# Attention features and a token/channel mixer on one core: the channel mix of batches 1 to 3 in stretches of 512 columns, batch 1's loads among the weights, half of batch 0's features on GpSimd

## The chip, the cores and the metric

One Trainium2 chip, of which the kernel uses 1 core. The metric is the device time of one execution in microseconds (us); of several runs the median is taken. In the names of the profile PE is TensorE (PEld its weight loads), DVE is VectorE, ACT is ScalarE, POOL is GpSimd and SP is SyncE, which here issues every DMA.

## The reference

```
def phi(x):                        # r = 8, so 64 features a head
    a = einsum('rd,bhsd->bhsr', S1, x); b = einsum('rd,bhsd->bhsr', S2, x)
    return (a[..., :, None] * b[..., None, :]).reshape(*x.shape[:-1], 64)
q_p, k_p = phi(q), phi(k)          # q, k, v: 4 batches, 4 heads, 1088 tokens, 32 wide
kv = einsum('bhsf,bhsd->bhfd', k_p, v); z = k_p.sum(axis=2)
x = (q_p @ kv) / (q_p @ z + 1e-6)  # per head, then heads side by side: (4, 1088, 128)
h = relu(x^T @ w_tok1) @ w_tok2    # token mix, 1088 -> 256 -> 1088
u = x + h^T
out = u + relu(u @ w_ch1) @ w_ch2  # channel mix, 128 -> 1536 -> 128
```

All is float32 in and out.

## The kernel before, in words

The weights come as doubles, 128 partitions wide, in pieces: nine tiles of `w_tok1` in pieces 00 to 04, `w_tok2` in 10 to 15, `w_ch1` in 20 to 22, `w_ch2` in 30 to 32. Each piece is turned into float32 words by five operations (`convert`, L256): ACT takes the magnitude (`.abs`, L266) and the tail (`.low`, L270), DVE clamps (L273), shifts (L277) and merges (L280), and POOL adds the tail (L284 where the result is kept as `whole`, L286 where not). Where a product needs full precision out of the faster fp32r matmuls, the words are split into a high and a low half (`divide_weight`, L361): ACT casts the high half (L368), POOL subtracts it to get the low one (L371). Products are then three matmuls: high by high, high by low, low by high.

A batch b goes through these steps. `K` (L385): k is projected on PE (L396), copied by ACT (L406) and multiplied into features `k_p` by DVE (L415), and summed against v on PE (L432) into `kvz`. `Q`: batch 0 makes its query features on PE (L510), with an ACT copy (L514) and a DVE product (L517) for each of six blocks (three stretches of columns, two pairs of heads). Batches 1 to 3 project on PE (L477), copy by ACT (L543), write rows to DRAM (L551), read them back broadcast into `qp` and `br` (L564, L567) and multiply the two on POOL (L577). `A` (mixing, L581): attention `x` on PE (L596), divided by DVE (L607 to L610), split for batches 1 to 3 by ACT (L616) and POOL (L620); first token product (L641 in batch 0, L647 later), relu, transposes; x transposed into PSUM (L672), onto which the second token product is added (L708 in batch 0, L712 later); the sum u is split by ACT into `uh` (L717) and by DVE into `ul` (L721). `U` (channel mix, L732): for a stretch of columns and each of 12 pieces e of the hidden width, three matmuls make `ps_h` (L747), ACT takes the relu as `hh` (L751), DVE the rest as `hl` (L754), and three matmuls add into `ps_o` (L760); at a stretch's end `o_sb` is rebuilt (L777), the sum added (L780) and stored (L783). The stretches are 384, 384 and 320 columns in each batch, so a batch has 3 x 12 x 6 = 216 of these matmuls.

PSUM is three pools of banks: three `ps_a` for all but the channel mix, three `ps_h`, two `ps_o`. `qp`, `br`, `k_sb`, `v_sb` and `k_p` have one buffer each, `q_sb` two; `uh` and `ul` hold a whole batch (1088 columns), two buffers of each.

The order of the instructions on every engine is set when the program is built, by a planner (`Plan.run`, L97): a list scheduler with its own cost for each operation, which takes of the operations that could start soonest the one with the longest chain of cost behind it (`level`), raised for a batch by `BOOST`. Each engine then runs its list strictly in order; a waiting instruction holds up all behind it. SP's list of DMAs is one queue of that kind. `LOADS` gives the order in which the loads of weights and of batch 0 are issued; the loads of the other batches follow behind. Where the planner sees an idle PE ahead it puts in matmuls on the identity (`fill`, L242) that nothing reads.

Of the kernel before, what the change touches and what calls it, by code (L numbers as in the profile page):

```python
# [207 lines left out]
def attn_mixer_kernel(ctx: ExitStack, tc: tile.TileContext, qT, kT, v1, s64, wt1, wt2, wc1, wc2, out):  # L208
    nc = tc.nc
    engines = {"dve": nc.vector, "pool": nc.gpsimd, "act": nc.scalar}  # L210
    bufs = {"c": 4, "tail": 4, "a_sb": 3, "ar": 2, "den": 2, "o_sb": 2, "q_sb": 2, "u": 2, "uh": 2, "ul": 2, "rec": 2, "hid": HID, "hh": HID, "hl": HID, "rows": 2, "ps_a": 3, "ps_h": 3, "ps_o": 2}
# [273 lines left out]
    def queries_on_pe(qp_hold):  # L485
# [16 lines left out]
        for g, (c0, cn) in enumerate(CHUNKS):  # L502
            for p in range(2):
                a_hold, b_hold, ar_hold = Hold("ps_a"), Hold("ps_h"), Hold("ar")
# [10 lines left out]

                def multiply(_, g=g, p=p, cs=cs, cn=cn):
                    nc.vector.tensor_tensor(qp[:, p, cs], t["ar", g, p][:, :cn], t[1, g, p][:, :cn], op=ALU.mult)  # L517
# [63 lines left out]
    def mixing(b, kvz_done, qp_done, qp_hold, boost):  # L581
# [115 lines left out]
        u_hold = Hold("u")  # L697
        u_done, second_done = [], []
        for i, (c0, cn) in enumerate(CHUNKS):
# [14 lines left out]
            def high(_, i=i, c0=c0, cn=cn):  # L714
                if i == 0:
                    box["uh", b], box["ul", b] = new("uh", [P, S], F32R), new("ul", [P, S], F32R)
                nc.scalar.copy(box["uh", b][:, c0:c0 + cn], t["u", i][:, :cn])  # L717

            def low(_, i=i, c0=c0, cn=cn):
                cs = slice(c0, c0 + cn)  # L720
                nc.vector.tensor_tensor(box["ul", b][:, cs], t["u", i][:, :cn], f32(box["uh", b][:, cs]), op=ALU.subtract)  # L721

            s = plan.add(f"{n}.w{i}", {"pe": 6 * (cn / 2.4 + 14) if b else 8 * (cn / 1.2 + 3)}, second, [m, residuals[i]] + [(is_split if b else is_whole)[1, 2 * i + f] for f in range(2)], (), [u_banks[i], hTs_hold], boost)
# [8 lines left out]
    def channel_mix(b, u_done, u_hold):  # L732
        segs = SEGS if not b else [(i, 0, NCH) for i in range(3)]
        o_holds = [Hold("ps_o") for _ in CHUNKS]
        outs = {}
        for i, e0, e1 in segs:
            c0, cn = CHUNKS[i]
            cs = slice(c0, c0 + cn)
            for e in range(e0, e1):
# [3 lines left out]
                def first(_, t=t, e=e, cs=cs, cn=cn):  # L743
                    h_ps = t["h"] = bank("ps_h")
                    uh, ul = box["uh", b], box["ul", b]
                    for m, (l, r) in enumerate(((0, uh), (0, ul), (1, uh))):
                        nc.tensor.matmul(h_ps[:, :cn], lhsT=part(2, at[2][e][0], l, at[2][e][1] * P, P), rhs=r[:, cs], start=(m == 0), stop=(m == 2))  # L747
# [106 lines left out]
```

## Time and profile before

| | us |
|---|---|
| median of 3 runs (lowest, highest) | 235.20 (234.39, 236.41) |
| profiled execution, its own time | 237.45 |
| its span, first to last instruction | 235.7 |
| PE, busy in the span | 225.1 |
| DVE, busy | 141.6 |
| ACT, busy | 116.9 |
| POOL, busy | 76.1 |

Times within the profile are counted from the span's start. The groups give the busy time of the instructions of one line and their mean duration; a PE instruction's duration runs from its start to the end of its way through the array, so that consecutive matmuls overlap and the time one adds to a stream is read from the distance of their starts (the chain of waits gives that). The waits name what ended an idle time; an engine's timeline gives its instructions in order. The granted TensorE clock is 1.000.

### The profile page before, as it was taken

What the parts mean: (1) busy time and instruction counts of PE and PEld (TensorE: products, weight loads), DVE (VectorE), ACT (ScalarE), POOL (GpSimd) and SP (SyncE); (2) the same over time, 40 slices, a digit from 0 to 9 for tenths busy, and PEclk for the clock granted to TensorE, in tenths of its full rate; (3) what the DMA queues carried; (4) which work ended last, traced back from release to release, by engine and by line L of the source; (5) the groups of instructions that cost most, each with busy time, mean ns of one, the idle gap of its engine ahead of it and who ended that gap; (6) DMA issues with size and microseconds to landing.
All of it is one profiled execution on the core that took longest, in us unless ns stands there. A gap on an engine that the chain in (4) does not pass through costs nothing.

```text
span 235.7 us, 4804 instructions
## 1 busy us (share of the span) xinstructions
PE 225.1 (95%) x1891; PEld 207.0 (88%) x1891; DVE 141.6 (60%) x280; ACT 116.9 (50%) x262; POOL 76.1 (32%) x76
## 2 busy tenths in 40 slices
PE   7799998799998999999998999999999999999994
PEld 7477765699886999989997999989999999999993
DVE  1598994987876356563656355548357456555653
ACT  4577379975623445443443344444443354444451
POOL 1224469898866410000066410100062611000000
PEclk9999999999999999999999999999999999999999
DMA  6999940269741000049951000015931000010000
GB/s 205 416 403 402 408 189 0 50 192 203 170 149 35 2 0 30 1 116 212 164 169 43 3 0 14 16 40 141 164 119 36 3 0 28 0 36 0 3 35 28
DMA packets 8279, 24.88 MB, mean 106 GB/s; under 512 B 960, under 2 KB 2624, under 8 KB 8256
## 3 DMA queue, kind: packets, MB, share of 16 engines
q1 hardware_dynamic: 8256, 24.57, 34.5%
q8 instruction: 15, 0.25, 0.5%
q14 instruction: 8, 0.07, 0.1%
HBM read 21.50 MB, written 3.06 MB: 104 GB/s over the span
## 4 chain that ended last, share of the span: by engine, by line
PE 57%; DMA 21%; DVE 7%; ACT 4%; SPq 4%; issue 4%; POOL 3%; POOLq 0%; DVEq 0%
PE ps_o L760 22%; PE ps_h L747 22%; DMA br<-rows 12%; DMA doubles<-wt 4%; PE ps_a L647 4%; DMA doubles<-wc 4%; PE ps_a L712 4%; PE ps_a L596 3%; DVE c L273 2%; POOL qp L577 2%; ACT halves L368 2%; SPq L567 1%; SPq L249 1%; PE ps_a L672 1%; DVE hl L754 1%
## 5 line engine op out<-in xcount | busy, mean ns | idle before, releaser
L754 DVE SCALAR_TENSOR_TENSOR hl<-ps_h,hh 128x384 fp32r<-128x384 f32 (+1 forms) x144 | 76.1, 533 | 63.2 <-ACT hh L751 62.6
L751 ACT ACTIVATE hh<-ps_h 128x384 fp32r<-128x384 f32 (+1 forms) x144 | 68.0, 474 | 66.9 <-PE ps_h L747 58.5
L747 PE MATMUL ps_h<-uh,halves 128*128 128x384 f32 (+1 forms) x288 | 93.9, 334 | 2.1 <-DVE hl L754 1.5
L760 PE MATMUL ps_o<-hh,halves 128*128 128x384 f32 (+1 forms) x288 | 72.7, 333 | 0.9 <-POOL halves L371 0.5
L747 PEld LDWEIGHTS ps_h<-uh,halves 128*128 128x128 f32 x288 | 53.8, 188 | 4.8 <-DVE hl L754 2.2
L760 PEld LDWEIGHTS ps_o<-hh,halves 128*128 128x128 f32 x288 | 50.3, 188 | 2.5 <-POOL halves L371 1.0
L747 PE MATMUL ps_h<-ul,halves 128*128 128x384 f32 (+1 forms) x144 | 47.2, 328 | 0.1
L760 PE MATMUL ps_o<-hl,halves 128*128 128x384 f32 (+1 forms) x144 | 47.2, 328 | 0.0
L577 POOL TENSOR_TENSOR qp<-qp,br 128x544 f32<-128x544 f32 x12 | 16.2, 1364 | 59.2 <-DMA br<-rows 33.4
L747 PEld LDWEIGHTS ps_h<-ul,halves 128*128 128x128 f32 x144 | 27.1, 189 | 0.5 <-DVE ul L721 0.3
L760 PEld LDWEIGHTS ps_o<-hl,halves 128*128 128x128 f32 x144 | 27.1, 188 | 0.1
L777 POOL TENSOR_TENSOR o_sb<-uh,ul 128x384 f32<-128x384 f32 (+1 forms) x12 | 11.6, 966 | 44.2 <-DVE ul L721 29.1
L284 POOL TENSOR_TENSOR whole<-c,tail 128x512 int32<-128x512 int32 (+3 forms) x11 | 11.8, 1080 | 19.7 <-DVE c L280 18.9
L266 ACT ACTIVATE c<-doubles 128x512 f32<-128x512 f32 (+3 forms) x17 | 10.2, 614 | 6.9 <-POOL whole L284 5.1
L273 DVE TENSOR_SCALAR c<-c 128x512 f32<-128x512 f32 (+3 forms) x17 | 11.9, 718 | 2.5 <-ACT c L266 2.5
L371 POOL TENSOR_TENSOR halves<-whole,halves 128x512 fp32r<-128x512 f32 (+3 forms) x11 | 11.9, 1098 | 0.7 <-ACT halves L368 0.7
L620 POOL TENSOR_TENSOR xl<-x,xh 128x384 fp32r<-128x384 f32 x9 | 9.0, 1011 | 9.3 <-ACT xh L616 9.3
L596 PEld LDWEIGHTS ps_a<-kvz,qp 128*64 128x64 f32 x288 | 9.2, 137 | 3.0 <-issue 1.9
L415 DVE TENSOR_TENSOR k_p<-ps_a,a_sb 128x1024 f32<-128x1024 f32 (+1 forms) x12 | 10.7, 949 | 1.3 <-ACT a_sb L406 1.3
L721 DVE TENSOR_TENSOR ul<-ps_a,uh 128x384 fp32r<-128x384 f32 (+1 forms) x12 | 6.4, 533 | 8.5 <-ACT uh L717 8.5
L596 PE MATMUL ps_a<-kvz,qp 128*64 128x66 f32 x288 | 10.4, 225 | 0.8 <-POOL qp L577 0.8
L277 DVE TENSOR_SCALAR ps_h<-c 128x512 int32<-128x512 int32 (+3 forms) x17 | 10.3, 612 | 0.1
(69 smaller groups left out, 243.7 us busy)
## 6 DMA issues: line engine op xcount, KB each, us to landing
qp<-rows SPq DMA_DIRECT2D x6, 544.0 KB
br<-rows SPq DMA_DIRECT2D x12, 272.0 KB
doubles<-wc SPq DMA_DIRECT2D x6, 512.0 KB
v_sb<-v SPq DMA_DIRECT2D x4, 594.0 KB
k_sb<-kT SPq DMA_DIRECT2D x4, 576.0 KB
q_sb<-qT SPq DMA_DIRECT2D x4, 544.0 KB
doubles<-wt SPq DMA_DIRECT2D x4, 512.0 KB
doubles<-wt SPq DMA_DIRECT2D x4, 384.0 KB
```

What stands on the lines that cost most here:

```text
L273: nc.vector.tensor_scalar(f32(t["c"]), f32(t["c"]), LEAST, MOST, op0=ALU.max, op1=ALU.min)
L277: nc.vector.tensor_scalar(t["ps"], t["c"], 3, 0x3FFFFFFF, op0=ALU.logical_shift_left, op1=ALU.bitwise_and)
L284: engines[e].tensor_tensor(dst(), t["c"], t["tail"], op=ALU.add)
L371: engines[e].tensor_tensor(halves[w, i][:, 1], f32(whole[w, i] if w < 2 else t["c"]), f32(halves[w, i][:, 0]), op=ALU.subtract)
L415: nc.vector.tensor_tensor(t["k_p"][:pn, t0 * H:t1 * H], a.unsqueeze(3).broadcast_to([pn, n, R, R]), t["sb", t0][:pn, :n].unsqueeze(2).broa ...
L577: engines[e].tensor_tensor(qp[:, p, cs], qp[:, p, cs], t["br"][:, p, cs], op=ALU.mult)
L596: nc.tensor.matmul(x_ps[c:c + 64, o:o + 2 * (D + 1)], lhsT=qp[:, p, s0 + c:s0 + c + 64], rhs=kvz_all[b % 2][:, p, :], start=True, stop=True,)
L747: nc.tensor.matmul(h_ps[:, :cn], lhsT=part(2, at[2][e][0], l, at[2][e][1] * P, P), rhs=r[:, cs], start=(m == 0), stop=(m == 2))
L751: nc.scalar.activation(t["hh"][:, :cn], t["h"][:, :cn], AF.Relu)
L754: nc.vector.scalar_tensor_tensor(t["hl"][:, :cn], t["h"][:, :cn], 0.0, f32(t["hh"][:, :cn]), op0=ALU.max, op1=ALU.subtract)
L760: nc.tensor.matmul(outs[i][:, :cn], lhsT=part(3, at[3][e][0], l, at[3][e][1] * P, P), rhs=r[:, :cn], start=(e == 0 and m == 0), stop=(e == ...
L777: engines[e].tensor_tensor(outs["sb", i][:, :cn], f32(box["uh", b][:, cs]), f32(box["ul", b][:, cs]), op=ALU.add)
```

## The change

Seven edits, of which the planner then makes a new order for all engines.

- **Stretches of 512.** Batch 0 keeps 384, 384 and 320. The 3264 columns of batches 1 to 3 are taken as one row and cut into 512 x 5, 448 and 256, so stretches run over the border of two batches. `uh`, `ul`, `hh`, `hl` and `o_sb` become tiles of 512 columns, five `uh` and five `ul` of them. A second-product chunk that lies in two stretches is split by two ACT and two DVE operations (`evict`), and a stretch that lies in two batches is stored by two DMAs.
- **Loads.** q1, k1 and v1 are issued among the weights (behind 30, 13 and 31) and not behind them.
- **GpSimd features.** Of the six blocks of batch 0's query features three, those of the second pair of heads, are multiplied by POOL. It can't read PSUM, so ACT copies both factors; `ar` has three buffers.
- **Single leads.** A table adds to or takes from the level of single operations.
- In batches 1 to 3 the three groups of the attention matmuls stand together as one step, behind the third transposition of the batch before.
- The planner's time for the first load, for a landing, and for batch 0's second product are other numbers.
- `u_done` is a list for each stretch, so a stretch waits for its own pieces alone.

The diff, cut to its core:

```diff
-LOADS = "00 q k 01 v 02 03 04 10 11 20 30 12 13 21 31 14 15 22 32".split()
+LOADS = "00 q0 k0 01 v0 02 03 04 10 11 20 30 q1 12 13 k1 21 31 v1 14 15 22 32".split()
+WIDE = 512
+def _spans():
+    spans = [((0, c0, cn),) for c0, cn in CHUNKS]
+    at = S
+    for n in (512, 512, 512, 512, 512, 448, 256):
...
+ON_POOL = {(0, 1), (1, 1), (2, 1)}
+LEAD = {
+    "A0.d2": -2500.0,
+    "A0.t2": -30000.0,
+    "A0.w1": 7000.0,
...
+    "K3.p": 27000.0,
...
+    "w21.lo": -111500.0,
+}
-            op.level += op.boost
+            op.level += op.boost + LEAD.get(op.name, 0.0)
-        dma, mode = 1680.0, 0
+        dma, mode = 2800.0, 0
-                op.end = dma + 1200
+                op.end = dma + (1200 if op.bytes > 100000 else 0)
-    bufs = {... "ar": 2, ... "u": 2, "uh": 2, "ul": 2, ...}
+    bufs = {... "ar": 3, ... "u": 5, "uh": 5, "ul": 5, ...}
+                def copy_b(_, g=g, p=p, cn=cn):
+                    t["br", g, p] = new("ar", [P, 384])
+                    nc.scalar.copy(t["br", g, p][:, :cn], t[1, g, p][:, :cn])
+                def multiply_both(_, g=g, p=p, cs=cs, cn=cn):
+                    nc.gpsimd.tensor_tensor(qp[:, p, cs], t["ar", g, p][:, :cn], t["br", g, p][:, :cn], op=ALU.mult)
...
+            elif g == 0:
+                attended = plan.add(f"{n}.x", {"pe": 18 * 117.0}, lambda _: [f(_) for f in attends], [kvz_done] + sum(qp_done.values(), []), x_banks, [qp_hold], boost, 1, order=free)
...
+        def evict(k, i, s, src, dst, cn):
+            def high(_):
+                if ("uh", k) not in box:
+                    box["uh", k], box["ul", k] = new("uh", [P, WIDE], F32R), new("ul", [P, WIDE], F32R)
+                nc.scalar.copy(box["uh", k][:, dst:dst + cn], t["u", i][:, src:src + cn])
...
-    def channel_mix(b, u_done, u_hold):
-        segs = SEGS if not b else [(i, 0, NCH) for i in range(3)]
+    def channel_mix(segs):
...
+                    uh, ul = box["uh", i], box["ul", i]
                     for m, (l, r) in enumerate(((0, uh), (0, ul), (1, uh))):
-                        nc.tensor.matmul(h_ps[:, :cn], lhsT=part(...), rhs=r[:, cs], start=(m == 0), stop=(m == 2))
+                        nc.tensor.matmul(h_ps[:, :cn], lhsT=part(...), rhs=r[:, :cn], start=(m == 0), stop=(m == 2))
...
+                for b, c0, m in SPANS[i]:
+                    def store(_, i=i, b=b, c0=c0, m=m, d0=d0):
+                        nc.sync.dma_start(out[b][:, c0:c0 + m], outs["sb", i][:, d0:d0 + m])
...
-            q_loaded[b + 1] = load_q(b + 1, [prev], BOOST[b + 1])
-            k_loaded[b + 1] = load_k(b + 1, [q_loaded[b + 1]], BOOST[b + 1])
-            v_loaded[b + 1] = prev = load_v(b + 1, [k_loaded[b + 1]], BOOST[b + 1])
+            for get, known in by_kind.values():
+                if b + 1 not in known:
+                    prev = known[b + 1] = get(b + 1, [prev], BOOST[b + 1])
```

What the planner made of it, at three places. First PE's list just ahead of batch 0's channel mix, which begins with the first row on `ps_h<-uh`. Lines of the changed kernel are other numbers: L438 and L474 are batch 1's key projection and sums (L396 and L432 before), L702 and L785 batch 0's token products, L733 and L742 transposes, L519 a query projection, L820 and L833 the channel mix. Before:

```order
L708 MATMUL ps_a<-whole_409,hTl 128x384
L708 MATMUL ps_a<-whole_414,hTl 128x384
L245 MATMUL ps_o<-ident 128x128 x5
L708 MATMUL ps_a<-whole_459,hTl 128x384
L708 MATMUL ps_a<-whole_468,hTl 128x384
L747 MATMUL ps_h<-uh,halves_456 128x384
```

Changed:

```order
L438 MATMUL ps_a<-s_c,k_sb 64x64 x18
L702 MATMUL ps_a<-whole_326,x 128x256 x2
L702 MATMUL ps_a<-whole_376,x 128x256
L286 MATMUL ps_o<-ident 128x128 x3
L742 MATMUL ps_a<-ident,h 128x128 x2
L733 MATMUL ps_a<-ident,x 128x128 x3
L785 MATMUL ps_a<-whole_409,hTl 128x384
L785 MATMUL ps_a<-whole_427,hTl 128x384
L733 MATMUL ps_a<-ident,x 128x128 x3
L474 MATMUL ps_a<-v_sb,k_p 64x66 x36
L785 MATMUL ps_a<-whole_479,hTl 128x384
L785 MATMUL ps_a<-whole_563,hTl 128x384
```

Batch 1's keys and sums, which stood among the first groups of the channel mix, now stand ahead of it; so does, some rows earlier, batch 1's query projection. `whole_468` and `whole_563` are the same piece of weights, 13.

Second DVE's list up to the merge of that piece (`c<-doubles_92`). Before:

```order
L280 SCALAR_TENSOR_TENSOR c<-doubles_89,ps_h 128x512
L277 TENSOR_SCALAR ps_h<-c 128x384 x2
L280 SCALAR_TENSOR_TENSOR c<-doubles_91,ps_h 128x384
L273 TENSOR_SCALAR c<-c 128x512
L280 SCALAR_TENSOR_TENSOR c<-doubles_92,ps_h 128x384
```

Changed:

```order
L321 SCALAR_TENSOR_TENSOR c<-doubles_91,ps_h 128x384
L457 TENSOR_TENSOR k_p<-ps_a,a_sb 128x1024 x2
L457 TENSOR_TENSOR k_p<-ps_a,a_sb 128x256
L314 TENSOR_SCALAR c<-c 128x384
L314 TENSOR_SCALAR c<-c 128x512 x2
L318 TENSOR_SCALAR ps_h<-c 128x384
L318 TENSOR_SCALAR ps_h<-c 128x512
L321 SCALAR_TENSOR_TENSOR c<-doubles_92,ps_h 128x384
```

Batch 1's key features, one clamp more and one shift of 512 more now stand ahead of that merge; three of batch 0's products (L517) are gone from the rows above.

Third POOL's list behind the add of that piece (`whole_563`), changed:

```order
L325 TENSOR_TENSOR whole_563<-c,tail 128x384
L327 TENSOR_TENSOR c<-c,tail 128x512 x2
L411 TENSOR_TENSOR halves_583<-c,halves_583 128x512
L327 TENSOR_TENSOR c<-c,tail 128x512
L411 TENSOR_TENSOR halves_626<-c,halves_626 128x512
L411 TENSOR_TENSOR halves_654<-c,halves_654 128x512
L327 TENSOR_TENSOR c<-c,tail 128x512
L411 TENSOR_TENSOR halves_690<-whole_156,halves_690 128x512
L411 TENSOR_TENSOR halves_724<-c,halves_724 128x512
L327 TENSOR_TENSOR c<-c,tail 128x512
L632 TENSOR_TENSOR qp<-qp,br 128x544
L411 TENSOR_TENSOR halves_771<-c,halves_771 128x512
```

The halves that are made from `c` are the channel mix's weights, those from `whole` the token mix's. Before, nine subtractions for the token weights (00 to 04 and 10 to 13) stood among and ahead of the channel weights' later pieces; now all but one stand behind them, and batch 1's feature products (L632, `qp<-qp,br`) stand among them.

More of the change, by code (lines that the diff above doesn't have):

```diff
@@ L210, in attn_mixer_kernel @@
     engines = {"dve": nc.vector, "pool": nc.gpsimd, "act": nc.scalar}
-    bufs = {"c": 4, "tail": 4, "a_sb": 3, "ar": 2, "den": 2, "o_sb": 2, "q_sb": 2, "u": 2, "uh": 2, "ul": 2, "rec": 2, "hid": HID, "hh": HID, "hl": HID, "rows": 2, "ps_a": 3, "ps_h": 3, "ps_o": 2}
+    bufs = {"c": 4, "tail": 4, "a_sb": 3, "ar": 3, "den": 2, "o_sb": 2, "q_sb": 2, "u": 5, "uh": 5, "ul": 5, "rec": 2, "hid": HID, "hh": HID, "hl": HID, "rows": 2, "ps_a": 3, "ps_h": 3, "ps_o": 2}
     const = ctx.enter_context(tc.tile_pool(name="const", bufs=1))
@@ L584, in mixing @@
         x_hold, xs_hold = Hold("x"), Hold("xs")
-        divided, split = [], []
+        divided, split, attends = [], [], []
+        x_banks = [Hold("ps_a") for _ in range(3)]
         for g in range(3):
-            ps = Hold("ps_a")
+            ps = x_banks[g]
             def attend(_, g=g):
@@ L712, in second @@
                         nc.tensor.matmul(u_ps[:, :cn], lhsT=t[l][:, f, :], rhs=part(1, 2 * i + f, r, 0, cn), start=False, stop=(k == 6), skip_group_check=True)
[L714 to L723, printed above, removed]
-            second_done.append(s)
-            hi = plan.add(f"{n}.uh{i}", act(cn), high, [s], [u_hold] if i == 0 else (), [u_banks[i]] + ([u_hold] if i else []), boost, order=u_done[:1])
-            u_done += [plan.add(f"{n}.ul{i}", dve(cn), low, [hi], (), [u_banks[i], u_hold], boost)]
-        return mixed, second_done, u_done, u_hold, residuals
+            s = plan.add(f"{n}.w{i}", {"pe": 6 * (cn / 2.4 + 14) if b else 4 * (cn / 1.2 + 3)}, second, [m, residuals[i]] + [(is_split if b else is_whole)[1, 2 * i + f] for f in range(2)], (), [u_banks[i], hTs_hold], boost)
+            second_done.append(s)
+            for k, parts in enumerate(SPANS):
+                d0 = 0
+                for pb, p0, pn in parts:
+                    lo, n_ = max(c0, p0), min(c0 + cn, p0 + pn) - max(c0, p0)
+                    if pb == b and n_ > 0:
+                        evict(k, i, s, lo - c0, d0 + lo - p0, n_)
+                    d0 += pn
+        return second_done, residuals
     chain = {"f": None, "s": None}
-    def channel_mix(b, u_done, u_hold):
-        segs = SEGS if not b else [(i, 0, NCH) for i in range(3)]
-        o_holds = [Hold("ps_o") for _ in CHUNKS]
-        outs = {}
+    def channel_mix(segs):
+        o_holds, outs = {}, {}
         for i, e0, e1 in segs:
-            c0, cn = CHUNKS[i]
-            cs = slice(c0, c0 + cn)
+            cn = sum(m for _, _, m in SPANS[i])
+            o_hold = o_holds.setdefault(i, Hold("ps_o"))
+            n = f"U{i}"
             for e in range(e0, e1):
@@ L762, in channel_mix @@
                 cost = 3 * (cn / 2.4 + 14)
-                n = f"U{b}"
-                f = plan.add(n + ".f", {"pe": cost}, first, [u_done[i], is_split[2, at[2][e][0]]], [ps], [u_hold], 0.0, 0, 2 * cost, [chain["f"]])
+                f = plan.add(n + ".f", {"pe": cost}, first, u_done[i] + [is_split[2, at[2][e][0]]], [ps], [u_holds[i]], 0.0, 0, 2 * cost, [chain["f"]])
                 chain["f"] = f
@@ L767, in channel_mix @@
                 m = plan.add(n + ".l", dve(cn), low, [m], (), [ps, hid])
-                s = plan.add(n + ".s", {"pe": cost}, second, [m, is_split[3, at[3][e][0]]], [o_holds[i]] if e == 0 else (), [hid] + ([o_holds[i]] if e else []), 0.0, 0, 2 * cost, [chain["s"]])
+                s = plan.add(n + ".s", {"pe": cost}, second, [m, is_split[3, at[3][e][0]]], [o_hold] if e == 0 else (), [hid] + ([o_hold] if e else []), 0.0, 0, 2 * cost, [chain["s"]])
                 chain["s"] = s
```

88 lines of the change are left out of this document (61 added, 27 removed).

## The prediction, made before the changed kernel ran

> **What bounds the kernel now.** First the page's busy times and shares of the chain, then the windows, cut where batch 0's channel mix begins (35.14) and where batch 1's first token product ends (80.7).
>
> ```profile
> PE 225.1 (95%) x1891; PEld 207.0 (88%) x1891; DVE 141.6 (60%) x280; ACT 116.9 (50%) x262; POOL 76.1 (32%) x76
> 0.00:35.14 35.14, 32.04 (x289) 24.21 (x289) 26.60 (x56) 21.02 (x47) 13.02 (x20) 1.00 0.88 339
> 35.14:80.89 45.75, 42.33 (x382) 36.72 (x381) 32.30 (x61) 27.96 (x65) 37.80 (x34) 1.00 0.41 103
> 80.89:232.40 151.51, 150.69 (x1225) 146.07 (x1224) 82.24 (x162) 67.90 (x152) 25.26 (x23) 1.00 0.22 53
> L245 PE MATMUL ps_o<-ident 128*128 128x128 f32 x50 | 8.7, 339 | 1.4 <-POOL ident masks.py:199 1.4
> GB/s 205 416 403 402 408 189 0 50 192 203 170 149 35 2 0 30 1 116 212 164 169 43 3 0 14 16 40 141 164 119 36 3 0 28 0 36 0 3 35 28
> ```
>
> Three stages. In the last, 151.5 us, PE is busy 150.7: matmuls alone set its length. In the middle one PE has holes and POOL is the fullest other engine, 37.8 of 45.75. In the first, PE is full only by name: 50 of its matmuls are filler (8.7 us), and DVE, 26.6 of 35.1 and without a rest from 10 us on, sets the pace. So the end moves by three things: PE's work behind 35.14, PE's waits there, and the moment at which the channel mix begins.
>
> **The change, part by part.** *Stretches of 512.* The chain of waits shows what one group of consecutive matmuls adds to PE's stream: 6 of 320 columns, 3 of 384, 18 of 256.
>
> ```profile
> 222.08 0.88 PE ps_h L747 x6
> 205.84 0.52 PE ps_h L747 x3
> 131.07 2.13 PE ps_a L647 x18
> ```
>
> That is 146.7, 173.3 and 118.3 ns each. From 320 to 384 a column costs 0.417 ns and 13.3 ns stay as a fixed part; so 512 should cost 226.7 and 448 200.0. Batches 1 to 3 pass each stretch in 72 matmuls. Before: 6 x 173.3 + 3 x 146.7 = 1480 ns; changed: 5 x 226.7 + 200.0 + 118.3 = 1452. Difference 28 ns x 72 = **-2.0 us**. The trace has no 512; along the line from 256 to 384 (0.43 a column) it is 228.3 and the gain 1.4; if the fixed part vanished at 512 the gain would be 6.8. I take 2.0, as 320 and 384 are the same instruction at the same place. DVE's and ACT's part of a group grows to some 0.68 and 0.60 us by the rows of 384 and 320, under PE's 1.36 for the pair of groups, so PE stays the longest.
>
> By the Trainium skill, page "TensorE: Matmul & The Clock Gate", section "Back-to-back issue gap", an isolated matmul costs N/2.4 + 2.5 ns, but a sustained stream at N = 512 runs at some 131 ns each. The first would make 384 columns 162.5 ns, and the row above says 173.3.
>
> *Work moved ahead of the channel mix.* Batch 1's query projection (L477), key projection (L396) and sums (L432) stood behind 35.14:
>
> ```profile
> 35.14 0.63 PE L747 MATMUL ps_h<-uh,halves 128*128 128x384 f32 x1
> 37.34 1.14 PE L477 MATMUL ps_a<-q_sb,s_rows 128*64 128x272 f32 x8
> 46.73 1.27 PE L396 MATMUL ps_a<-s_c,k_sb 128*64 128x64 f32 x36
> 50.65 2.32 PE L432 MATMUL ps_a<-v_sb,k_p 128*64 128x66 f32 x72
> ```
>
> 1.14 + 1.27 + 2.32 = 4.7. Their loads now come among the weights and PE does them where it did filler: **-4.7 us**, if the first stage doesn't grow. (Batch 2's query and key projections come forward into the middle stage; that only changes places.) The three loads are some 1.7 MB, 4 us at the 403 GB/s of the row above, and make later weights as much later. That costs nothing: all loads are over when GB/s falls to 0 (slice 7 of 5.9 us, from 35 on), and five of the six channel pieces got their add on POOL behind 33.3 (L286 x5 in POOL's groups below), so they lay waiting.
>
> *The start of the channel mix.* It waits for piece 13: merge on DVE, add on POOL, second token product on PE.
>
> ```profile
> 10.22 0.55 DVE L517 TENSOR_TENSOR qp<-ar,ps_h 128x384 f32<-128x384 f32 x1 [1.91 <-PE ps_h L510]
> 15.74 0.48 DVE L517 TENSOR_TENSOR qp<-ar,ps_h 128x320 f32<-128x320 f32 x1
> 10.69 0.42 DVE L273 TENSOR_SCALAR c<-c 128x512 f32<-128x512 f32 x1
> 11.75 2.68 DVE L415 TENSOR_TENSOR k_p<-ps_a,a_sb 128x1024 f32<-128x1024 f32 x3
> 27.49 2.13 DVE L273 TENSOR_SCALAR c<-c 128x512 f32<-128x512 f32 x2
> 32.72 0.54 DVE L280 SCALAR_TENSOR_TENSOR c<-doubles,ps_h 128x384 int32<-128x384 int32 x1
> 33.19 0.68 DVE L277 TENSOR_SCALAR ps_h<-c 128x512 int32<-128x512 int32 x1
> 27.25 2.15 POOL L284 TENSOR_TENSOR whole<-c,tail 128x384 int32<-128x384 int32 x2 [2.94 <-DVE c L280]
> ```
>
> The merge starts at 32.72; DVE's list ahead of it loses three products (2 x 0.55 + 0.48 = 1.6) and gains batch 1's key features (2.68), a clamp (0.42) and a shift (0.68): 2.2 us more. To that come waits. Two clamps at 27.49 took 2.13 where alone they take about 0.8: they stood behind POOL's adds at 27.25. The change puts three products of POOL, about 1.0 us each, into this stage, and three ACT copies (0.42 to 0.48) ahead of words that DVE wants. I put 1.1 us on that: **+3.3 us**. From below: nothing, if the 2.2 go where DVE waited anyway (the rows show 1.9 at 10.22 and 1.3 at 27.49). From above: each product holds a clamp for its whole 1.0 and the copies stand in line, 2.2 + 3.0 + 1.4 = 6.6.
>
> The Trainium skill, page "SBUF — State Buffer", section "Who interferes with whom", has the rule that speaks against GpSimd features: DVE in a two-port mode and GpSimd lock each other out for a whole instruction. By this, the trace agrees at 27.49, and the dear end would be the right one.
>
> *Waits of the middle stage.*
>
> ```profile
> 38.90 0.44 PE L760 MATMUL ps_o<-hh,halves 128*128 128x384 f32 x1 [0.42 <-ACT hh L751]
> 39.86 0.45 PE L760 MATMUL ps_o<-hh,halves 128*128 128x384 f32 x1 [0.53 <-POOL halves L371]
> 43.90 0.44 PE L747 MATMUL ps_h<-uh,halves 128*128 128x384 f32 x1 [1.33 <-DVE hl L754]
> 73.54 0.41 PE L747 MATMUL ps_h<-uh,halves 128*128 128x320 f32 x1 [0.60 <-ACT uh L717]
> 69.11 0.92 PE L596 MATMUL ps_a<-kvz,qp 128*64 128x66 f32 x24
> 74.55 1.62 PE L596 MATMUL ps_a<-kvz,qp 128*64 128x66 f32 x48
> 70.26 1.63 PE L708 MATMUL ps_a<-whole,hTl 128*128 128x320 f32 x4 [0.23 <-POOL whole L284]
> 80.60 0.28 PE L647 MATMUL ps_a<-halves,xl 128*128 128x256 f32 x1
> 125.39 0.81 PE L596 MATMUL ps_a<-kvz,qp 128*64 128x66 f32 x20 [0.76 <-POOL qp L577]
> ```
>
> From 35.14 to the next start after 80.60 (80.7) are 45.6 us. In it lie 48 groups of 384 (25.0), 4 of 320 (1.8), the 4.7 above, second product (1.6), attention (0.92 + 1.62), first token product (27 x 0.118 = 3.2): 38.8. So 6.8 are waits, one small transposition and what alternating shapes cost. In the new POOL list the channel weights' halves come ahead of the token weights', so the waits at 39.86 and 43.90 and their like shrink; but the second query projection now wants a PSUM bank that `ul` of the second stretch gives back, behind five conversions on DVE, about 1.8 us, and the first output group again waits for the half of piece 30, about 0.5. With 1.4 for transposition and shapes 3.7 stay: **-3.1 us** (between 0, the sum unchanged, and -5). The wait at 125.39 goes, since batch 2's reads are now issued as soon as batch 1's attention is done, some 35 us ahead of use: **-0.8**.
>
> What hides the rest: POOL. Behind the add of piece 13 it has, up to batch 1's feature products, one add of 384, five adds and four halves of 512, one half of a token piece; up to batch 1's first `xl`, 21 us more.
>
> ```profile
> L371 POOL TENSOR_TENSOR halves<-c,halves 128x512 fp32r<-128x512 f32 x6 | 7.7, 1292 | 0.9 <-ACT halves L368 0.9
> L286 POOL TENSOR_TENSOR c<-c,tail 128x512 int32<-128x512 int32 x5 | 6.4, 1289 | 0.2
> L371 POOL TENSOR_TENSOR halves<-whole,halves 128x512 fp32r<-128x512 f32 x4 | 5.3, 1339 | 0.7 <-ACT halves L368 0.7
> L371 POOL TENSOR_TENSOR halves<-whole,halves 128x384 fp32r<-128x384 f32 x4 | 4.1, 1066 | 0.0
> L577 POOL TENSOR_TENSOR qp<-qp,br 128x544 f32<-128x544 f32 x4 | 5.5, 1382 | 2.7 <-issue 2.3 <-DMA br<-rows 0.4
> L620 POOL TENSOR_TENSOR xl<-x,xh 128x384 fp32r<-128x384 f32 x3 | 3.0, 1009 | 2.6 <-ACT xh L616 2.6
> ```
>
> From the merge's end at 36.6 that is 1.1 + 6.4 + 5.2 + 1.3 = 14.0 and some 0.9 of waits: feature products due at 51.5, first `xl` done at 72.8. PE comes there at 38.4 + 32.9 (the 38.8 less 4.7, less the token product and one group, with batch 2's two projections for 2.4) + 3.7 = 75.0. POOL is 2.2 us early: nearly a second bound.
>
> **The sum**: -2.0 - 4.7 - 3.1 - 0.8 + 3.3 = -7.3 us against the span of 235.7, so 228.4. The profiled execution took 237.45 with what lies around its span, but the runs' median is 235.20; taken off that, **227.9 us**. The last stretch is 256 and not 320; its end (one DVE add, one store) I leave as it is.
>
> **Rivals.** (1) *The front slips further*: start +6.6, waits unchanged but for the 0.8. Then -2.0 - 4.7 - 0.8 + 6.6 = -0.9: 234.3, no measurable change. For it: DVE has no rest there and the port waits are real; against: the dear end needs each product to hit a clamp. (2) *Batch 1's feature products hold POOL's list*. They stand ahead of piece 32's half and of all token halves, and their reads on SP stand behind the load of v2, which waits for batch 1's sums.
>
> ```profile
> 48.54 0.58 SPq L564 DMA_DIRECT2D qp<-rows  x1
> 53.01 0.34 SPq L249 DMA_DIRECT2D v_sb<-v  x1
> 60.41 1.36 POOL L577 TENSOR_TENSOR qp<-qp,br 128x544 f32<-128x544 f32 x1 [0.42 <-DMA br<-rows]
> 66.71 2.67 POOL L577 TENSOR_TENSOR qp<-qp,br 128x544 f32<-128x544 f32 x2 [2.29 <-issue]
> ```
>
> Before, 11.9 us passed from issue to first use. From some 37.3, when the sums are done, that gives 49.2, due 51.5. Past 53.7 (51.5 and POOL's 2.2) each us costs one, and past 61.0 the gain is gone; if they took twice their time and a little, to 64, it is 10.3: 238.2, slower than before by 1.3%. For it: POOL's list is strictly in order, and the second pair of reads took 18.2 us. Against: the second pair is due 6 us behind the first. (3) *The changed order helps nothing but the moved work*: waits stay at 6.8, start +3.3: -2.0 - 4.7 - 0.8 + 3.3 = -4.2: 231.0. (4) *The fixed part of a matmul doesn't show at 512*: the stretches give 6.8 and not 2.0: 223.1. Against it: 320 and 384 both carry it. The Trainium skill's section named above would have nearly that (2.5 ns left), and its 131 ns would take far more off; the trace's 173.3 for 384 speaks against both.
>
> **How the numbers follow.** Chances: forecast 0.66, rival 1 0.10, rival 2 0.07, rival 3 0.16, rival 4 0.01. A run of this kernel tells about 1% from no change (232.8 and below is faster, above 237.6 slower). The forecast, rival 3 and 4 are faster, 0.83, with 0.02 of rival 1; rival 2 is half slower (0.04), half same. So faster 0.85, same 0.11, slower 0.04. The range: down by the start at no cost and the waits at -5 gives 222.7, both together are unlikely, 223.5; up to rival 3 and halfway to rival 1, 232.5.
>
> **What would show it.** Right: matmuls of 512 at 227 ns each; the first on `ps_h<-uh` at about 38.4; L438 and L474 ahead of it; batch 1's token product done near 78.2; behind it PE without holes. Wrong: a start past 41, POOL waiting for `br<-rows` past 54, or 512 columns at 235 ns and more, which would eat the gain of the stretches.

## The result, and the profile after

| | before | changed | forecast |
|---|---|---|---|
| median, us | 235.20 | 227.33 (227.18 to 227.35, 4 runs) | 227.9 (223.5 to 232.5) |
| profiled execution, us | 237.45 | 227.31 | |
| its span, us | 235.7 | 225.5 | 228.4 |

The ratio is 0.9665, with a 95% interval of 0.962 to 0.9711. A second set of runs beside other kernels gave 227.19 and 0.9634 (0.96 to 0.9668); one of its six executions took 432.66 us, with matmuls of 512 columns 446 ns apart, and is left out of the ratio. The total came out as forecast; its terms did not.

The changed kernel's busy times, and its windows, cut where batch 0's channel mix begins (37.17) and where batch 1's first token product ends (74.90; the columns are the stretch, its length, then PE, PEld, DVE, ACT and POOL busy, granted clock, DMA share, GB/s):

```profile
PE 217.6 (96%) x1735; PEld 187.6 (83%) x1735; DVE 135.4 (60%) x256; ACT 113.1 (50%) x246; POOL 78.6 (35%) x77
0.00:37.17 37.17, 33.16 (x393) 25.77 (x393) 29.19 (x60) 25.53 (x59) 17.71 (x25) 1.00 0.90 345
37.17:74.90 37.73, 36.99 (x305) 34.41 (x304) 29.44 (x58) 25.26 (x60) 34.98 (x31) 1.00 0.47 127
74.90:222.30 147.40, 147.40 (x1042) 127.39 (x1040) 76.34 (x139) 62.28 (x128) 25.88 (x22) 1.00 0.18 48
```

The front grew by 2.0 us, the middle shrank from 45.75 to 37.7, the last stage from 151.5 to 147.4. PE has no hole left behind 74.90, as forecast (the forecast had this end of the token product near 78.2), and POOL is busy for 93% of the middle stage, against 83% before.

Next PE's timeline around the start of the mix (start, length, instruction, how many, and in brackets an idle time with what ended it):

```profile
21.16 1.14 PE L519 MATMUL ps_a<-q_sb,s_rows 128*64 128x272 f32 x8
27.44 1.27 PE L438 MATMUL ps_a<-s_c,k_sb 128*64 128x64 f32 x36
33.82 2.32 PE L474 MATMUL ps_a<-v_sb,k_p 128*64 128x66 f32 x72
36.07 1.56 PE L785 MATMUL ps_a<-whole,hTl 128*128 128x384 f32 x4
37.17 0.63 PE L820 MATMUL ps_h<-uh,halves 128*128 128x384 f32 x1
38.92 1.14 PE L519 MATMUL ps_a<-q_sb,s_rows 128*64 128x272 f32 x8
44.37 0.44 PE L820 MATMUL ps_h<-uh,halves 128*128 128x384 f32 x1 [0.74 <-DVE hl L827]
```

Batch 1's query projection, key projection and sums (L519, L438, L474) lie ahead of 37.17, and they and the second token product run right up to it: at the start PE itself is what was waited for. DVE's timeline has the merge of piece 13 (the first of the two at 33.99) and the first `ul`, which ends at 35.6; POOL's has that piece's add, over at 35.6 as well. Both are 1.6 us ahead of the start. The other rows are DVE's clamps between 19 and 25 us, and on POOL the three new products (L564) and the adds beside those clamps:

```profile
19.44 1.14 DVE L314 TENSOR_SCALAR c<-c 128x256 f32<-128x256 f32 x2
22.55 1.51 DVE L314 TENSOR_SCALAR c<-c 128x384 f32<-128x384 f32 x2
33.99 1.14 DVE L321 SCALAR_TENSOR_TENSOR c<-doubles,ps_h 128x384 int32<-128x384 int32 x2
35.05 0.55 DVE L768 TENSOR_TENSOR ul<-ps_a,uh 128x384 fp32r<-128x384 f32 x1
12.21 1.00 POOL L564 TENSOR_TENSOR qp<-ar 128x384 f32<-128x384 f32 x1 [2.62 <-ACT ar L557]
15.21 1.02 POOL L564 TENSOR_TENSOR qp<-ar 128x384 f32<-128x384 f32 x1 [1.99 <-ACT ar L557]
17.65 2.51 POOL L325 TENSOR_TENSOR whole<-c,tail 128x512 int32<-128x512 int32 x2 [0.18 <-DVE c L321]
20.68 0.87 POOL L564 TENSOR_TENSOR qp<-ar 128x320 f32<-128x320 f32 x1 [0.52 <-ACT ar L557]
22.71 1.06 POOL L325 TENSOR_TENSOR whole<-c,tail 128x384 int32<-128x384 int32 x1 [0.19 <-DVE c L321]
34.61 1.00 POOL L325 TENSOR_TENSOR whole<-c,tail 128x384 int32<-128x384 int32 x1 [2.74 <-DVE c L321]
```

The chain of waits gives the price of the new stretches, three matmuls of 512 and then six of 448:

```profile
190.55 0.70 PE ps_h L820 x3
199.57 1.23 PE ps_h L820 x6
```

That is 233 and 205 ns a matmul; the starts of consecutive 512 lie 234 ns apart (median of 360). The forecast had 226.7 and 200.0.

PE's named waits behind the start, first of before, then of the changed kernel (total, times, longest):

```profile
PE ps_h L747 <- DVE hl L754: 1.5, 2, 1.3
PE ps_a L596 <- POOL qp L577: 0.8, 1, 0.8
PE ps_h L747 <- ACT uh L717: 0.6, 1, 0.6
PE ps_o L760 <- POOL halves L371: 0.5, 1, 0.5
PE ps_o L760 <- ACT hh L751: 0.4, 1, 0.4
PE ps_a L708 <- POOL whole L284: 0.2, 1, 0.2
```

```profile
PE ps_h L820 <- DVE hl L827: 0.7, 1, 0.7
```

4.0 us became 0.7. POOL's timeline shows the two marks of rival 2, batch 1's first feature product and its `xl`:

```profile
50.07 1.36 POOL L632 TENSOR_TENSOR qp<-qp,br 128x544 f32<-128x544 f32 x1
69.51 2.99 POOL L676 TENSOR_TENSOR xl<-x,xh 128x384 fp32r<-128x384 f32 x3
```

The product didn't wait for its reads and started at 50.07 (due 51.5). The first of the three `xl` was done at 70.5 (forecast 72.8); PE came to it at 71.6 (forecast 75.0), so POOL was only 1.1 us ahead, nearly the second bound that the forecast had seen.

**An account for all kernels.** To compare kernels whose lists differ, I count each matmul behind the first one on `ps_h<-uh` at its kind's usual distance of starts (fp32r of 512, 448, 384, 320, 256 columns: 234, 204, 174, 147, 117 ns; the rest likewise). What the time up to the last matmul holds beyond that is "rest": named waits, and many small delays, above all where kinds of matmul alternate. The rest of "attention split" and of the first "384, 384, 320" also holds what a lowered clock cost. From the profiled executions, us:

| kernel | median | start | work behind | rest behind | end | span |
|---|---|---|---|---|---|---|
| before | 235.2 | 35.1 | 184.4 | 12.4 | 3.7 | 235.7 |
| changed | 227.3 | 37.2 | 180.7 | 4.1 | 3.6 | 225.5 |
| old loads | 229.8 | 32.7 | 186.2 | 5.4 | 3.6 | 227.9 |
| features on DVE | 230.0 | 34.8 | 186.2 | 3.6 | 3.6 | 228.1 |
| no leads | 231.8 | 34.1 | 186.2 | 6.0 | 3.6 | 229.9 |
| these three undone | 232.3 | 34.8 | 186.2 | 5.9 | 3.6 | 230.4 |
| and 384, 384, 320 | 232.3 | 34.5 | 185.7 | 6.3 | 4.2 | 230.6 |
| 384 late | 228.0 | 37.1 | 180.2 | 5.0 | 3.7 | 226.1 |
| attention split | 231.4 | 37.9 | 180.7 | 8.0 | 3.6 | 230.2 |
| 384, 384, 320 | 246.6 | 38.3 | 180.2 | 23.0 | 4.1 | 245.6 |
| same, one lead less | 231.8 | 38.8 | 180.2 | 6.9 | 4.1 | 230.0 |

Before's profiled execution was 2.25 us above its median; if that lies in its rest, the rest was 10.1 in a usual run. A start is good to some 0.8 us: four profiled executions with the same lists ahead of it (384 late, changed, the changed kernel with a stream behind its end, attention split) have it at 37.1, 37.2, 37.5 and 37.9.

By distances of starts, eight single waits of 0.36 to 1.49 us make 5.9 us of before's rest; they are the seven named above and one on `ul`. With "384, 384, 320" and the three edits undone, three such waits make 1.4, in the changed kernel one makes 1.0. So of the 8.3 that the rest fell by, some 4.8 are single waits that went.

### The profile page after: what moved, and what is told of

Read it like the earlier page. It is cut to its first block, busy times and chain, and to the rows that moved or that the text cites. A ratio compares the mean times of both kernels' runs of the same rounds, so it can differ in the third digit from the quotient of the medians.

```text
span 225.5 us, 4427 instructions
## 1 busy us (share of the span) xinstructions
PE 217.6 (96%) x1735; PEld 187.6 (83%) x1735; DVE 135.4 (60%) x256; ACT 113.1 (50%) x246; POOL 78.6 (35%) x77
## 4 chain that ended last, share of the span: by engine, by line
PE 79%; DVE 8%; DMA 7%; SPq 1%; issue 1%; POOL 1%; ACT 1%; DVEq 0%
PE ps_o L833 31%; PE ps_h L820 31%; PE ps_a L708 4%; DMA doubles<-wt 4%; PE ps_a L789 4%; PE ps_a L652 3%; DMA qp<-rows 3%; PE ps_a L474 2%; DVE c L314 2%; DVE c L321 2%; DVE ps_h L318 1%; PE ps_a L733 1%; SPq L290 1%; DVE k_p L457 1%; PE ps_a L438 1%
## 5 line engine op out<-in xcount | busy, mean ns | idle before, releaser
L827 DVE SCALAR_TENSOR_TENSOR hl<-ps_h,hh 128x512 fp32r<-128x512 f32 (+4 forms) x120 | 73.0, 611 | 61.6 <-ACT hh L824 60.7
L824 ACT ACTIVATE hh<-ps_h 128x512 fp32r<-128x512 f32 (+4 forms) x120 | 64.2, 536 | 69.2 <-PE ps_h L820 56.2
L820 PE MATMUL ps_h<-uh,halves 128*128 128x512 f32 (+4 forms) x240 | 86.2, 366 | 0.7 <-DVE hl L827 0.7
L833 PE MATMUL ps_o<-hh,halves 128*128 128x512 f32 (+4 forms) x240 | 67.4, 362 | 0.0
L820 PEld LDWEIGHTS ps_h<-uh,halves 128*128 128x128 f32 x240 | 44.9, 188 | 7.4 <-DVE hl L827 1.2
L833 PEld LDWEIGHTS ps_o<-hh,halves 128*128 128x128 f32 x240 | 42.9, 188 | 5.6
L833 PE MATMUL ps_o<-hl,halves 128*128 128x512 f32 (+4 forms) x120 | 43.4, 361 | 0.0
L820 PE MATMUL ps_h<-ul,halves 128*128 128x512 f32 (+4 forms) x120 | 43.2, 360 | 0.0
L632 POOL TENSOR_TENSOR qp<-qp,br 128x544 f32<-128x544 f32 x12 | 16.2, 1369 | 44.7 <-DMA br<-rows 44.7
L833 PEld LDWEIGHTS ps_o<-hl,halves 128*128 128x128 f32 x120 | 22.5, 188 | 3.4 <-DVE hl L827 0.5
L820 PEld LDWEIGHTS ps_h<-ul,halves 128*128 128x128 f32 x120 | 22.6, 188 | 2.5
L849 POOL TENSOR_TENSOR o_sb<-uh,ul 128x512 f32<-128x512 f32 (+4 forms) x10 | 11.3, 1131 | 36.5 <-DMA outT<-o_sb 22.7
L311 ACT ACTIVATE tail<-doubles 128x512 int32<-128x512 uint32 (+3 forms) x17 | 10.4, 618 | 1.2 <-DMA doubles<-wt 1.2
```

The lines of the kernel that those rows point to most:

```text
L632: engines[e].tensor_tensor(qp[:, p, cs], qp[:, p, cs], t["br"][:, p, cs], op=ALU.mult)
L824: nc.scalar.activation(t["hh"][:, :cn], t["h"][:, :cn], AF.Relu)
L827: nc.vector.scalar_tensor_tensor(t["hl"][:, :cn], t["h"][:, :cn], 0.0, f32(t["hh"][:, :cn]), op0=ALU.max, op1=ALU.subtract)
L833: nc.tensor.matmul(outs[i][:, :cn], lhsT=part(3, at[3][e][0], l, at[3][e][1] * P, P), rhs=r[:, :cn], start=(e == 0 and m == 0), stop=(e == ...
L849: engines[e].tensor_tensor(outs["sb", i][:, :cn], f32(box["uh", i][:, :cn]), f32(box["ul", i][:, :cn]), op=ALU.add)
```

## The experiments

Theory A: fp32r matmuls cost by the column, so stretches of 512 give nothing; the gain is work moved ahead of the mix and waits that went with the new order. Rival B: wide stretches are worth the forecast's 2 us, and 234 ns comes from something beside them.

**The changed kernel again**, as control.

> The changed kernel itself, once more beside the two runs with other stretches, so that all three have the same runs of before to stand against. Both theories: 227.3 us, ratio 0.967.

227.19 us, 0.9634 (0.96 to 0.9668): as expected.

**The price of a width.** The edit, behind the kernel's end (`stream(n, 24)` issues 24 fp32r matmuls of n columns):

```diff
+    for n in (512, 448, 384, 320, 256, 512):
+        stream(n, 24)
...
+    for _ in range(10):
+        nc.scalar.copy(d1, src_ps)
+        nc.vector.tensor_scalar_add(d2, src2_ps, 1.0)
+    stream(512, 24)
```

> The changed kernel, and behind its end 24 matmuls each of 512, 448, 384, 320, 256 and again 512 columns on an idle chip (fp32r, the same tiles, new weights for each), then 24 of 512 while ScalarE and VectorE copy 512 columns out of two other banks over and over. The added matmuls are extra work that nothing reads. Theory A (the size alone): distances of starts of 234, 204, 173, 147, 117 and 234 ns on the idle chip, and 234 beside the copies. Rival C (the 512 are slowed by the readers of PSUM): about 227 or less on the idle chip and 234 or more beside the copies.

The chain for the six idle streams together, and PE's timeline for the one beside the copies:

```profile
223.32 26.69 PE ps_a L894 x144
```

```profile
250.31 5.76 PE L894 MATMUL ps_a<-uh,halves 128*128 128x512 f32 x24
```

Within the 144 the mean distances were 233.3, 204.5, 176.4, 146.5, 117.9 and again 233.4 ns, and 24 of each make 26.7 us, as the row has it. Beside the copies 24 x 233 ns and one drain give the 5.76. Rival C is out: it is the size alone, 0.456 to 0.46 ns a column from 256 on, and a fixed part of some 2 ns at most. (By the Trainium skill, page "TensorE: Matmul & The Clock Gate", section "Back-to-back issue gap", an isolated matmul of 512 takes 216 ns and a sustained stream 131 each; neither is what this stream shows.)

**Stretches undone in two ways.**

```diff
-    for n in (512, 512, 512, 512, 512, 448, 256):
+    for n in (384, 384, 320) * 3:
```

> The changed kernel with batches 1 to 3 cut into 384, 384 and 320 again; all else as in the change. Theory A (a column costs 0.455 ns at every width, a matmul has no fixed part that a wider one saves): 72 x (6 x 173.4 + 3 x 146.8 - 5 x 234.0 - 204.4 - 116.7) ns = -0.8 us against the changed kernel, so 226.5 us, and about 0.99 us more or less if the planner's new list has other waits. Rival B (the prediction's: 13.3 ns fixed, 512 at 226.7 when nothing disturbs it, or some other good of fewer and wider steps): undoing costs 2.0 us, so 229.3 us.

The second, with `(384,) * 8 + (192,)`:

> The changed kernel with batches 1 to 3 cut into 384 x 8 and 192. Theory A: 8 x 173.4 + 192 x 0.456 = 1474.8 ns a pass against 1491.5, x 72 = -1.2 us, so 226.1 us; the matmuls of 192 columns stand at 87 to 88 ns. Rival B: 8 x 173.4 + 93.4 = 1480.6 against the 1452 that 512 should have cost, so +2.0 us, 229.4 us; the matmuls of 192 columns stand at 93 ns.

246.58 us (ratio 1.0463, 1.0425 to 1.05) and 247.71 us (1.0506, 1.0466 to 1.0546), slower than before, and nothing that either theory said. PE's timeline of the first:

```profile
63.24 1.01 PE L820 MATMUL ps_h<-uh,halves 128*128 128x384 f32 x2 [14.33 <-POOL halves L411]
```

And POOL's, just ahead of it:

```profile
54.60 2.61 POOL L632 TENSOR_TENSOR qp<-qp,br 128x544 f32<-128x544 f32 x2
57.17 4.79 POOL L411 TENSOR_TENSOR halves<-whole,halves 128x512 fp32r<-128x512 f32 x5
61.92 1.26 POOL L411 TENSOR_TENSOR halves<-c,halves 128x512 fp32r<-128x512 f32 x1
```

Other stretches gave other levels, and the planner made another list. PE waits 14.3 us for the half of a channel piece (`halves<-c`), which stands on POOL behind batch 1's feature products and five token halves (`halves<-whole`). The second has a 14.3 us wait on the same line. As a test of widths both are worthless. One thing more they show. The chain of the second, in its last stretch of 192 columns:

```profile
241.39 0.34 PE ps_h L820 x3
```

That is 113 ns a matmul (mean distance of starts 112), not 87: at 192 columns it is only some 5 ns cheaper than at 256.

**The same without one lead.** Piece 21's low half had a lead of -111500.

```diff
-    "w21.lo": -111500.0,
```

> The re-cut into 384, 384 and 320, with the one lead of -111500 on the low half of piece 21 left out. Theory L (the 14 us were this half's place in GpSimd's list, behind batch 1's feature products and the token halves, and not the stretches): the wait on the halves goes, and with it the restart of the clock behind it, 14 us and some 3 us: 228 us, between 226.5 and 231 by what the new list has of small waits. Rival M (narrower stretches by themselves drain PE faster than GpSimd can follow): the hole comes back at the next half that GpSimd has late, 240 us or more.

231.82 us, 0.984 (0.9804 to 0.9876). Theory L holds for the wait: in the planner's new list that half stands some sixteen rows earlier, the wait is gone, and with it 14.8 us. The time lies 0.8 above its range, though, and 4.5 us above the changed kernel (start 1.6 later, rest 2.8 more; its waits on `hl` are 1.6 against 0.7).

**Narrow stretches late, the lists ahead unchanged.**

```diff
-    for n in (512, 512, 512, 512, 512, 448, 256):
+    for n in (512, 512, 384, 384, 384, 384, 384, 320):
-                cost = 3 * (cn / 2.4 + 14)
+                cost = 3 * (cn / 2.4 + (98 / 8 if i > 2 else 14))
```

> The changed kernel with batches 1 to 3 cut into 512 x 2, 384 x 5 and 320: five matmuls of 512, one of 448 and one of 256 become two of 512, five of 384 and one of 320. The early stretches stay and the planner's constant for a step of the channel mix is set so that all levels keep their sums, so the engines' lists are those of the changed kernel through batch 1's attention: the wait of 14 us that the two full re-cuts opened can't come. Theory A (the size alone, by the idle stream: 234, 174, 147): 2 x 234 + 5 x 174 + 147 = 1485 against 1491.5 ns a pass, x 72 = -0.5 us: 226.8 us, with PE without holes in the last stage. Rival B (fewer and wider steps are worth something): slower than the changed kernel by 1 us and more, 228.3 or above.

228.04 us, 0.9672 (0.9638 to 0.9705); the control's 0.9634 (0.96 to 0.9668) is from another set of runs, and the two intervals overlap. The work is 0.5 us less, as theory A had it, but the rest 0.9 us more and the end 0.2: neither theory's number. So wide stretches don't pay by their matmuls, but may be worth up to 0.9 us by fewer small delays. The pair below puts that at nothing.

**The three other edits, one at a time.** No leads (`LEAD = {}`):

> The changed kernel without the table of single leads; stretches of 512, the new order of loads and GpSimd's features stay. The planner then puts batch 1's key projection and sums behind the start of the channel mix again (3.6 us; the query projection as well, 1.1). Theory A (most of the gain is work moved ahead of the mix, and that hangs on the leads): 4.7 us back behind the start, the start some 2 us earlier, waits of the middle stage up by 1 to 4: 231 to 234 us. Rival D (the leads are polish, the loads and GpSimd's features carry the gain): 227 to 229 us.

231.83 us, 0.9835 (0.9795 to 0.9876). Old loads:

```diff
-LOADS = "00 q0 k0 01 v0 02 03 04 10 11 20 30 q1 12 13 k1 21 31 v1 14 15 22 32".split()
+LOADS = "00 q0 k0 01 v0 02 03 04 10 11 20 30 12 13 21 31 14 15 22 32".split()
```

> The changed kernel with batch 1's three loads behind the weights again; leads, GpSimd's features and stretches stay. The key projection, its sums and the query projection can't come ahead then. Theory A: +4.7 us behind the start, the start some 2 us earlier, waits up by 0 to 3: 230 to 233 us. Rival E (what is moved ahead only changes places with DVE's extra work in the first stage, so the loads are worth nothing): 227 to 228 us.

229.78 us, 0.9753 (0.9706 to 0.9799). Features on DVE (`ON_POOL = set()`):

> The changed kernel with all six blocks of batch 0's query features on VectorE; loads, leads and stretches stay. The planner then leaves batch 1's key projection, sums and query projection behind the start. Theory A: as with the old loads (start 4.5 us earlier, 4.4 us of work more behind it, 1.3 us more of waits), and the three products, 1.6 us, delay VectorE in the first stage: 230 to 231.5 us. Rival P (the products only change places between two engines with slack): 227 to 228 us.

229.96 us, 0.976 (0.9731 to 0.9789). No leads lies in theory A's range (231 to 234), the other two 0.2 us and less under the lower end of theirs (230); rivals D, E and P are out. Taking out any one edit costs 2.4 to 4.5 us, and in all three lists batch 1's sums stand behind the start again. But the account tells more than I had expected. PE's timelines, first with old loads, then with the features on DVE:

```profile
31.68 1.28 PE L286 MATMUL ps_o<-ident 128*128 128x128 f32 x10
32.71 0.42 PE L820 MATMUL ps_h<-uh,halves 128*128 128x384 f32 x1
```

```profile
32.83 2.17 PE L286 MATMUL ps_o<-ident 128*128 128x128 f32 x18
34.76 0.42 PE L820 MATMUL ps_h<-uh,halves 128*128 128x384 f32 x1
```

With the moved work gone the mix starts at 32.7, 4.5 us before the changed kernel's, and PE does filler just ahead of it. So moving 5.5 us (batch 1's 4.2, and four more matmuls of batch 0's second product, which then come ahead too) cost 4.5 of start: a net of 1.0. And the features on POOL don't delay the start. With all three edits undone it is 34.75; features and leads without the new loads make it 32.71, 2.0 earlier, features and new loads without the leads 34.10, 0.65 earlier, which is within the 0.8 that a start is good to.

**All three undone, with wide and with old stretches.**

> Old loads, no leads, all features on VectorE; stretches of 512, the attention in one step, buffers and the planner's other numbers stay. Theory W (stretches of 512 give nothing, and the small waits behind the start go by the rest of the change): the same as the next kernel within 1 us, both at 229 to 232 us. Rival V (the wide stretches take the small waits away): 229 to 231 us, and the next kernel 2 us and more above it.

> Old loads, no leads, all features on VectorE, and batches 1 to 3 in 384, 384 and 320; only the attention in one step, the buffers, a stretch's wait for its own pieces alone and the planner's other numbers are left of the change. Theory W: 229 to 232 us, well under before's 235.4. Rival V: 234 us and more, near before.

232.25 us, 0.986 (0.9831 to 0.9888), and 232.34 us, 0.987 (0.9838 to 0.9902). Theory W holds, though both times lie 0.3 us above its range: the wide stretches are worth 0.1 us here, and 3.3 us of the gain are there without them, the loads, the features and the leads. What is left in the second is the attention in one step, the buffers, a stretch's wait for its own pieces alone, and the planner's other numbers.

**The attention in three steps.**

```diff
-            if not b:
+            if True:
                 attended = plan.add(f"{n}.x{g}", {"pe": 6 * 117.0}, attend, ...)
```

> The changed kernel with the attention of batches 1 to 3 in three steps for the planner again, each with its own bank, as before; all else as in the change. Theory S (the small waits that went from PE's list behind the start, some 6 us, went largely because PE changes less often between the two kinds of matmuls): 1 to 2 us back, 228.3 to 229.3 us. Rival T (three steps land beside each other anyway): 227.0 to 227.8 us.

231.39 us, 0.9821 (0.9783 to 0.9859). That is more than theory S wanted, and not for its reason. PE's list was hardly split: the attention of batches 1 and 3 still runs as 72 matmuls in a row, as rival T had it, and only batch 2's stands in two parts, where before all three did:

```profile
104.20 0.87 PE L652 MATMUL ps_a<-kvz,qp 128*64 128x66 f32 x24
111.31 1.63 PE L652 MATMUL ps_a<-kvz,qp 128*64 128x66 f32 x48
```

What cost the time is elsewhere. DVE, POOL and PE of this kernel around 55 us:

```profile
53.44 2.79 DVE L314 TENSOR_SCALAR c<-c 128x320 f32<-128x320 f32 x2
```

```profile
52.10 1.32 POOL L411 TENSOR_TENSOR halves<-c,halves 128x512 fp32r<-128x512 f32 x1
53.35 1.40 POOL L632 TENSOR_TENSOR qp<-qp,br 128x544 f32<-128x544 f32 x1
54.66 1.39 POOL L411 TENSOR_TENSOR halves<-whole,halves 128x512 fp32r<-128x512 f32 x1
```

```profile
57.15 0.69 PE L820 MATMUL ps_h<-uh,halves 128*128 128x384 f32 x1 [2.25 <-DVE hl L827]
```

The new list put two clamps ahead of an `hl`. In the changed kernel the two clamps of 320 stand apart and take 0.41 and 0.59; the first:

```profile
53.79 0.41 DVE L314 TENSOR_SCALAR c<-c 128x320 f32<-128x320 f32 x1
```

Here the two took 2.79 while POOL ran without a gap up to 56.05, and each ended 0.18 us behind the POOL instruction beside it (54.75 and 56.05). PE waited 2.25 for the `hl` behind them. (By the Trainium skill, page "SBUF — State Buffer", section "Who interferes with whom", a DVE `tensor_scalar` in a two-port mode and GpSimd lock each other out for a whole instruction; by this rule, the trace agrees.) Then the clock, in this kernel's windows:

```profile
56.00:58.00 2.00, 0.85 (x3) 0.85 (x4) 2.00 (x6) 0.00 (x0) 0.48 (x2) 0.72 0.04 10
58.00:60.00 2.00, 2.00 (x8) 2.00 (x7) 1.31 (x3) 0.49 (x1) 1.74 (x2) 0.50 0.01 4
60.00:62.00 2.00, 2.00 (x13) 2.00 (x12) 0.56 (x1) 1.30 (x3) 1.94 (x2) 0.93 0.00 0
```

It was granted at 0.72, 0.50 and 0.93: 2 x (0.28 + 0.50 + 0.07) = 1.7 us lost. Wait 2.25, clock 1.7 and a start that came 0.7 later make 4.7, all of the 4.7 between the two spans. The 0.7 is this execution's: ahead of the start the lists are the changed kernel's on PE, DVE, ACT and POOL. So one split costs nothing that shows, and undoing this edit alone brings none of before's single waits back; what three splits cost, which is what theory S is about, this run doesn't show. The traces bound one part of it. Before, PE changes ten times between the channel mix and the attention, in the changed kernel six times, at about 0.1 us each by distances of starts: 0.4 us.

## Why the prediction was right, term by term

The total was right, -7.3 forecast and -7.9 by the medians, and the direction of every stage too. That it came so near was luck: of its five terms one held roughly, and the errors of the others cancelled.

- **Stretches of 512, -2.0: wrong.** The step that failed is "from 320 to 384 a column costs 0.417 ns and 13.3 ns stay as a fixed part". The fixed part was rounding. A chain row of three matmuls, 0.52 us, can be 171.7 to 175.0 ns each, and the row of six, 0.88, 145.8 to 147.5; the line through them gives 512 anything from 220 to 233. Measured distances of 174, 147 and 234 leave no fixed part worth the name: the stretches cost 72 x (1491 - 1485) ns = 0.4 us more work. Their own effect on the time is between 0.1 (the pair with all else undone) and 0.9 us (late stretches). The text named 235 ns as what would prove it wrong, but gave the mechanism a range that ended at a gain of 1.4.
- **Work moved ahead, -4.7: right in kind, and mis-sized by the drain.** All three steps came ahead. By distances of starts they are 4.2 us; the lengths of rows, 1.14, 1.27 and 2.32, each hold the way of the last matmul through the array as well.
- **Start of the mix, +3.3: +2.0 measured, and by another path.** The merge of piece 13 came 1.3 later (33.99 against 32.72) and not 3.3: ahead of it DVE worked 1.7 more, where 2.2 were counted, and waited 0.5 less. The 1.1 of port waits had the wrong sign. None of POOL's three products held a clamp. The clamps that were held (0.87 for the one of 256 at 19.44, 1.24 for the one of 512 behind 22.55) ran beside POOL's adds, as those at 27.49 had before. Ahead of the merge clamps took 1.4 us more than the 0.29 to 0.42 that each takes alone, against 1.8 before; in the whole kernel they took 9.0 against 11.9. By the experiments features on POOL with the leads are worth -2.0, and the moved work +4.5. And in the end it was PE's own list, not DVE's, that set the start: piece 13's add was over at 35.6, and PE, which had no hole from 32.0 on (there it had waited 0.2 for `hTl`), came to its product at 36.8.
- **Waits of the middle stage, -3.1, and of A2's attention, -0.8: far too small.** The rest behind the start fell by 8.3 us in the profiled executions, by about 6 in usual ones. Of the mechanisms named, the bank of the second query projection didn't hold PE (the row at 38.92 followed without a bracket) and the 0.76 wait went. But 6.1 of the 8.3 (some 4 of 6 in usual runs) are gone with loads, features, leads and stretches all undone, so none of these four is needed for most of it. I had priced the attention in one step, five buffers of `uh` and `ul`, the separate waits of stretches and the planner's numbers at nothing.

  Which of these it is stays open. The attention's step isn't needed for it where all the other edits are in place (undone there, it brought none of before's waits back), but that run split only one batch; the other three were not tried.
- **Sum.** -2.0 should have been +0.4 or nothing, +3.3 was +2.0, -4.7 was about -4.2 and -3.9 was about -6.
- **Rivals.** Rival 1 failed at 37.2. Rival 2 did not happen in the changed kernel, but its mechanism is real: POOL's list, strictly in order, held PE for 14.3 us when another half was late. Rival 3 is the opposite of what happened. Rival 4 had the wrong end: the fixed part was already absent at 384.

## What to carry to other kernels

Read the price of an instruction from a long run of it, and carry its rounding through before extrapolating: a line through 0.52 and 0.88 us can't tell a fixed part of 13 ns from none. Work that is moved into a stage that another engine paces isn't free there. Here 4.5 of the 5.5 us that it saved came back as a later start, and only the account "start + work behind + rest" shows that. Where a planner makes the lists, undoing an edit tests the new list as much as the edit: compare the lists first, and undo so that they stay the same up to the place that is asked about.

## What the runs showed that was not expected

- fp32r matmuls at 233 to 234 ns for 512 columns, 118 for 256, 112 for 192: by the column down to 256, with little more saved at 192.
- Matmuls of 448 lay 204 ns apart in the changed kernel and on the idle chip, but 200 in four kernels with other lists (old loads, features on DVE, no leads, all three). I don't know why; differences between widths under 2% aren't settled by this.
- A PE wait of 2.25 us was followed by a granted clock of 0.50, at a cost of 1.7 us more (as much as 3.4 us at half). Of the six executions of that kernel (attention split) one had a mean clock of 1.000 all the same (230.04 us). The wait of 14.3 us was followed by the same fall: the mean of the 16 us behind it was 0.89.

```profile
38.00:66.00 28.00, 12.94 (x65) 10.54 (x64) 10.84 (x22) 12.41 (x29) 24.93 (x21) 0.76 0.51 115
66.00:82.00 16.00, 16.00 (x82) 15.75 (x80) 8.87 (x18) 7.21 (x15) 5.40 (x6) 0.89 0.04 13
```

  The wait of 0.74 us in the changed kernel left the clock at 1.00. The Trainium skill's page "TensorE: Matmul & The Clock Gate", section "Why this matters for your kernels", warns of idle gaps over about 3 us; here one of 2.25 was enough.
